# Retention and a bilinear feed-forward layer: seven short products instead of twelve long ones for three more pairs of output tiles

## The chip, the cores and the metric

One core of one Trainium2 chip runs the whole program. The metric is the device time of one execution in microseconds (us), as the median of several runs. The engines are TensorE (PE, matmuls; its weight loads are shown as PEld), VectorE (DVE), ScalarE (ACT), GpSimd (POOL) and SyncE (SP, which here only issues transfers).

## What is computed

A decaying recurrence over the sequence (a linear attention) for each batch and head, then a feed-forward layer that multiplies two projections with each other before the output projection:

```
state = gamma * state + k[t] (outer) v[t]           # 4 batches, 8 heads, 768 positions, 64 wide
y[t]  = (q[t] @ state) / sqrt(64)
x     = y, with the heads side by side              # (3072, 512)
out   = ((x @ w_a) * (x @ w_b)) @ w_out             # 512 -> 1536 -> 512, float32 out
```

## The kernel before

The 3072 rows are 24 tiles of 128 positions. They are gathered into eight groups, `TILES = [4, 2, 2, 2, 2, 4, 4, 4]`, called J = 0 to 7. For a group the kernel computes the hidden rows in twelve blocks `ft` of 128 of the 1536 hidden columns: `ffn_a` (four matmuls with w_a into a PSUM bank, which ACT casts to `asb`), `ffn_g` (four matmuls with w_b into another bank, which DVE multiplies with `asb` into `ht`). Then the output of the group is made, by tile (`ffn_out`) or by pair of tiles (`ffn_fast`).

`ffn_out(J, i)` (line 617) makes one tile: twelve matmuls with 512 columns of w_out each, a copy of the bank by ACT into `osb`; after the second tile of a pair `osb` is put on the list `held`, which the next `store()` sends out.

`ffn_fast(J, u)` (line 663) makes a pair of tiles u at once by Strassen's scheme in Winograd's form: with the rows of the pair and the two halves of w_out as a 2x2 matrix, seven products of half the width replace eight. A product is six matmuls of 256 columns (`product`, line 652). Its left side is either hidden rows as they are ("h") or one of four sums of hidden rows ("s", tiles `hsum`, made by `add` on DVE); its right side is either w_out (`wo_bf`) or one of four combinations of its quarters (`wt_bf`, made by `combine_o` on DVE). In the text the products are called by their left sides: h00, h10, h11 (no sum) and s1, s0, s2, s3. The before runs them in the order h00, h10, s1, s0, s2, s3, h11. Three banks are used: R1 takes h00, s1, s2, h11 one upon the other; R6 takes h10; R5 takes s0, s3. Between products that go into one bank ACT copies a state of it into `snap`. So s2 cannot begin before ACT has copied s1's result, nor s3 before s0's.

In the before `FAST = (2, 3, 5, 6, 7)`: groups 2, 3, 5, 6 and 7 run `ffn_fast`, groups 0, 1 and 4 run `ffn_out`. The sums of a fast group are made during its own blocks by the table `adds`.

The recurrence is laid between these. `turn(new, old)` (line 393) makes on PE the chunk states and scores of two new tiles and the results y of two older ones: some 130 small matmuls. Its chunk states go to one of the three banks of the pool `psff`, which the blocks and the output use too (lines 274 to 299); DVE adds them up (`sums`, four instructions, the first and third of which read that bank), and only then is the bank free. The casts of its results into `xt` (ACT, line 383) and of the states into `gst` (ACT, line 199) are put on a list `later`, from which `catch_up(n)` issues n at a time; the masking of scores (DVE, line 320) is on a list `unmasked`, issued by `mask_now(n)`. `casts(t)` scales keys and queries of a tile on POOL (line 236), then issues their transposing transfer on SP and the loads of the next two tiles. The table `ahead` says where each of these stands: at a block (J, ft) or at an output tile (J, "o", i); `visit` issues it.

The order of all instructions of an engine is fixed by the order in which the code is written (`seq`). A buffer of a pool is given to the next tile in the order in which the earlier ones are done in that order. SBUF tiles `wstage` (four of tag wa, four of tag wb) hold in turn the raw weights, then `osb`, `hsum` and `snap`.

Of the kernel before, what the change touches and what calls it, by code (L numbers as in the profile page):

```python
# [9 lines left out]
F32 = mybir.dt.float32  # L10
# [6 lines left out]
FAST = (2, 3, 5, 6, 7)  # L17
# [7 lines left out]
def kernel(  # L25
# [10 lines left out]
    nc = tc.nc  # L36
# [533 lines left out]
    def ffn_a(J, ft, c0=0, c1=None):  # L570
# [5 lines left out]
        for kt in range(KT):  # L576
            for b0, b1 in parts(J, ft, c0, c1, NFT):
# [6 lines left out]
    def ffn_g(J, ft, c0=0, c1=None):  # L584
# [3 lines left out]
        for kt in range(KT):  # L588
            for b0, b1 in parts(J, ft, c0, c1, NFT):
# [5 lines left out]
    def ffn_ab(J, ft):  # L595
        if ft > 1:
            store()
        ffn_a(J, ft)
        ffn_g(J, ft)
        catch_up(TILES[J] // 2)  # L600
        mask_now(1)
# [38 lines left out]
    def add(J, which, f0, f1):  # L640
        if J not in hsum:
            hsum[J] = [wstage.tile([P, NH, 2, P], BF16, tag="w" + "ab"[i % 2], name="hsum") for i in range(4)]
        s = [x[:, f0:f1, : TILES[J] // 2] for x in hsum[J]]
        x, y, op = {
            0: (lambda: rows(J, 0, 1, f0, f1), lambda: rows(J, 1, 1, f0, f1), ALU.add),
            1: (lambda: s[0], lambda: rows(J, 0, 0, f0, f1), ALU.subtract),
            2: (lambda: rows(J, 0, 0, f0, f1), lambda: rows(J, 0, 1, f0, f1), ALU.subtract),
            3: (lambda: rows(J, 1, 0, f0, f1), lambda: s[1], ALU.subtract),
# [14 lines left out]
    def ffn_fast(J, u):  # L663
        osb, dst = placed[J, u] = place(J, u)
        ends = J == len(TILES) - 1 and u == TILES[J] // 2 - 1
        snap = wstage.tile([P, 3, DH], F32, tag="w" + "ba"[u % 2], name="snap")
# [3 lines left out]

        R1 = bank()
        product(R1, J, u, ("h", 0, 0), (0, 0), True)
        seq(nc.scalar.copy(snap[:, 0], R1[:, :DH]))  # L673
        catch_up(2)
        R6 = bank()
        product(R6, J, u, ("h", 1, 0), (0, 2), True)
        seq(nc.vector.tensor_tensor(osb[:, 0, :DH], R6[:, :DH], snap[:, 0], op=ALU.add))
        mask_now(1)
        catch_up(1)
        store()  # L680
        product(R1, J, u, ("s", 1), (1, 1), False)
        seq(nc.scalar.copy(snap[:, 1], R1[:, :DH]))
# [8 lines left out]
        if ends:  # L691
            seq(nc.sync.dma_start(out=dst[:, 1, DH:], in_=osb[:, 1, DH:]))
        product(R5, J, u, ("s", 3), (0, 3), False)
        seq(nc.vector.tensor_tensor(osb[:, 0, DH:], R5[:, :DH], snap[:, 1], op=ALU.add))
        mask_now()
        if ends:
            seq(nc.sync.dma_start(out=dst[:, 0], in_=osb[:, 0]))
        catch_up(1)
        product(R1, J, u, ("h", 1, 1), (1, 3), False)
        seq(nc.scalar.copy(osb[:, 1, :DH], R1[:, :DH]))  # L700
        if J < len(TILES) - 2:
            held.append((dst, osb))
        elif ends:
# [126 lines left out]
    def visit(*at):  # L830
        for fn, *what in ahead.pop(at, []):
            fn(*what)
# [56 lines left out]
```

## Time and profile before

| what | us |
|---|---|
| median of 3 runs (222.60, 224.06, 227.06) | 224.06 |
| the profiled execution | 223.43 |
| its span, from the first to the last instruction | 221.5 |
| PE busy in it | 213.6 (96%) |
| DVE busy | 132.1 (60%) |
| ACT busy | 94.6 (43%) |
| POOL busy | 81.2 (37%) |
| mean granted TensorE clock | 0.997 |

The profiled execution took 1.93 us more than its span. A line of the timeline has the start in us from the span's start, the length in us, the engine, the line of the kernel, the operation, the tiles (written <- read), the shape and how many such instructions in a row are merged; in brackets stands the idle time of the engine before it and what ended it. Matmuls are pipelined, so the length of a merged row reaches over the start of the next; the time that a stretch takes on PE is read from start to start. The outputs stand at these places: groups 0 and 1 from 51.2 to 68.9 us, group 2 from 80.8, group 3 from 97.6, group 4 from 114.5, group 5 from 143.1, group 6 from 178.4, group 7 from 208.5.

### The profile page before, as it was taken

The numbers are of one execution on the slowest core, as the hardware profiler recorded it, in microseconds if no ns is written. First come the engines' busy times: TensorE is split into PE (matmuls) and PEld (weight loads), VectorE is DVE, ScalarE is ACT, GpSimd is POOL, SyncE is SP. The second block draws the span as 40 slices with busy tenths as digits, with TensorE's granted clock in tenths as the row PEclk, the third lists the DMA queues.
The fourth block names the chain that finished last, engine by engine and source line by source line (L and its number), as shares of the span: only waits on it lengthen the run. The fifth ranks groups of instructions, "written<-read, shape, count | busy, mean of one in ns | idle before, by whom it ended". The sixth has DMA issues, their size and how long they took to land.

```text
span 221.5 us, 6783 instructions
## 1 busy us (share of the span) xinstructions
PE 213.6 (96%) x2809; PEld 149.4 (67%) x2809; DVE 132.1 (60%) x299; ACT 94.6 (43%) x220; POOL 81.2 (37%) x107
## 2 busy tenths in 40 slices
PE   8799999999999999999999999998999999999993
PEld 7578888885456888888875445576445488444682
DVE  2783556648615885787574358875357882355731
ACT  3775244342527445445465333625332633333231
POOL 6557798682734535054351606345000000000000
PEclk9999999999999999999999999999999999999998
DMA  6999999998998999997998979599400002200022
GB/s 175 344 377 382 368 293 376 345 203 165 220 265 185 211 211 222 133 227 201 211 142 188 229 160 232 116 249 164 195 0 3 0 3 95 98 0 1 0 98 95
DMA packets 94830, 39.76 MB, mean 180 GB/s; under 512 B 76112, under 2 KB 91728, under 8 KB 94800
## 3 DMA queue, kind: packets, MB, share of 16 engines
q1 hardware_dynamic: 94656, 39.20, 71.0%
q8 instruction: 22, 0.36, 0.7%
q10 hardware_dynamic: 144, 0.13, 0.2%
q14 instruction: 8, 0.07, 0.1%
HBM read 28.31 MB, written 6.29 MB: 156 GB/s over the span
## 4 chain that ended last, share of the span: by engine, by line
PE 85%; DMA 5%; ACT 3%; DVE 3%; POOL 1%; issue 1%; SPq 0%; ACTq 0%; POOLq 0%; DVEq 0%
PE g L590 28%; PE a L578 28%; PE o L660 13%; PE o L627 9%; DMA kf<-in_k_dram 3%; DMA out_dram<-osb 2%; ACT xt L383 1%; POOL kqb L236 1%; PE y L356 1%; PE at L314 1%; PE y L368 1%; DVE ht L593 1%; PE st L284 1%; DVE hsum L650 1%; PE tp L436 1%
## 5 line engine op out<-in xcount | busy, mean ns | idle before, releaser
L593 DVE TENSOR_TENSOR ht<-g,asb 128x256 bf16<-128x256 f32 (+1 forms) x98 | 53.8, 549 | 55.2 <-PE g L590 46.6
L590 PE MATMUL g<-xt,wb_bf 128*128 128x256 bf16 (+1 forms) x432 | 77.9, 308 | 0.1
L578 PE MATMUL a<-xt,wa_bf 128*128 128x256 bf16 (+1 forms) x432 | 77.6, 308 | 0.1
L582 ACT CAST asb<-a 128x256 bf16<-128x256 f32 (+1 forms) x98 | 46.2, 473 | 66.5 <-PE a L578 65.4
L590 PEld LDWEIGHTS <-wb_bf 128*128 128x128 bf16 x432 | 42.1, 98 | 20.6 <-issue 0.3
L578 PEld LDWEIGHTS <-wa_bf 128*128 128x128 bf16 x432 | 41.7, 98 | 20.1
L236 POOL TENSOR_TENSOR kqb<-kf,ktab 128x512 bf16<-128x512 f32 x21 | 22.8, 1088 | 39.3 <-DMA kf<-in_k_dram 30.8
L236 POOL TENSOR_TENSOR kqb<-qf,qtab 128x512 bf16<-128x512 f32 x21 | 22.5, 1071 | 6.1 <-DMA qf<-in_q_dram 5.8
L660 PEld LDWEIGHTS <-hsum 128*128 128x128 bf16 x192 | 18.6, 98 | 4.7 <-issue 1.7
L627 PE MATMUL o<-wo_bf,ht 128*128 128x512 bf16 x96 | 21.6, 379 | 0.0
L201 POOL CAST vb<-vf 128x512 bf16<-128x512 f32 x24 | 14.7, 623 | 17.1 <-DMA vf<-in_v_dram 11.2
L660 PE MATMUL o<-wt_bf,hsum 128*128 128x256 bf16 x144 | 17.7, 272 | 1.5 <-ACT snap L673 0.8
L627 PEld LDWEIGHTS <-ht 128*128 128x128 bf16 x96 | 9.2, 98 | 10.3
L660 PEld LDWEIGHTS <-ht 128*128 128x128 bf16 x144 | 13.7, 97 | 3.0 <-issue 0.2
L298 DVE TENSOR_TENSOR sums<-st,sums 128x256 f32<-128x256 f32 x30 | 12.7, 424 | 1.6
L199 ACT CAST gst<-sums 128x256 bf16<-128x256 f32 x33 | 12.5, 419 | 0.5 <-DVE sums L296 0.3
L650 DVE TENSOR_TENSOR hsum<-ht 128x256 bf16<-128x256 bf16 (+1 forms) x36 | 12.0, 339 | 0.4
L320 DVE TENSOR_TENSOR aT<-at,mask 128x512 bf16<-128x512 f32 x18 | 12.0, 680 | 0.0
L660 PE MATMUL o<-wo_bf,ht 128*128 128x256 bf16 x96 | 11.8, 273 | 0.0
L630 ACT COPY osb<-o 128x512 f32<-128x512 f32 x8 | 4.7, 586 | 12.1 <-PE o L627 11.4
L383 ACT CAST xt<-y 128x512 bf16<-128x512 f32 x16 | 8.7, 594 | 1.4 <-PE y L368 1.4
L700 ACT COPY osb<-o 128x256 f32<-128x256 f32 x8 | 3.0, 372 | 12.2 <-PE o L660 12.2
(83 smaller groups left out, 178.5 us busy)
## 6 DMA issues: line engine op xcount, KB each, us to landing
out_dram<-osb SPq DMA_DIRECT2D x11, 512.0 KB, 3.7
kf<-in_k_dram SPq DMA_DIRECT2D x18, 256.0 KB, 4.1
qf<-in_q_dram SPq DMA_DIRECT2D x36, 128.0 KB, 3.7
vf<-in_v_dram SPq DMA_DIRECT2D x18, 256.0 KB, 4.2
wsta<-in_moe_w_a_dram SPq DMA_DIRECT2D x6, 512.0 KB, 7.6
wstb<-in_moe_w_b_dram SPq DMA_DIRECT2D x6, 512.0 KB, 7.7
wsto<-in_moe_w_out_dram SPq DMA_DIRECT2D x6, 512.0 KB, 9.3
kf<-in_k_dram SPq DMA_DIRECT2D x3, 512.0 KB, 6.0
```

Of the source, the lines that this page charges most:

```text
L199: seq(nc.scalar.copy(dst, src))
L201: seq(engine.tensor_copy(dst, src))
L236: seq(eng.tensor_tensor(dst, src, tab, op=ALU.mult))
L298: seq(nc.vector.tensor_tensor(new, u[c][:, s], old, op=ALU.add))
L320: unmasked.append(lambda r=r: seq(nc.vector.tensor_tensor(aT[n][:, r].rearrange("p s h d -> p (s h) d"), at[:, r].rearrange("p s h d -> p ...
L578: seq(nc.tensor.matmul(a[:, b0 - c0 : b1 - c0], wa_bf[:, kt, fs], xcols(J, kt, b0, b1), start=(kt == 0 and b0 == c0), stop=(kt == KT - 1 a ...
L582: seq(nc.scalar.copy(asb, a))
L590: seq(nc.tensor.matmul(g[:, b0 - c0 : b1 - c0], wb_bf[:, kt, fs], xcols(J, kt, b0, b1), start=(kt == 0 and b0 == c0), stop=(kt == KT - 1 a ...
L593: seq(nc.vector.tensor_tensor(ht[J][:, ft, c0:c1], g, asbs.pop((J, ft, c0)), op=ALU.mult))
L627: seq(nc.tensor.matmul(o, ht[J][:, ft, i * P : (i + 1) * P], wo_bf[:, f, 2 * r : 2 * r + 2, :].rearrange("p a d -> p (a d)"), start=(ft == ...
L650: seq(nc.vector.tensor_tensor(s[which], x(), y(), op=op))
L660: seq(nc.tensor.matmul(R[:, :DH], lhs, (wo_bf, wt_bf)[w][:, f, m, :], start=(first and f == 0), stop=(f == NH - 1), skip_group_check=True))
```

## The change

Five things, all in the order and kind of instructions; what is computed stays the same but for rounding.

1. `ffn_fast` also makes the second pair of group 0 (tiles 2, 3), the pair of group 1 and the pair of group 4. Only the first pair of group 0 keeps `ffn_out`.
2. In every fast pair but the last of all, h11 is made third, into a bank of its own (R4), before any product with a sum; ACT copies it into a fourth part of `snap`. The last DVE instruction on R1 then writes both halves of a row block at once (128x512, with the bank read twice). The ACT copy of the last product falls away.
3. The sums for groups 0 and 1: four `add` of 128x768 behind the first pair of group 0 (they share their tiles with group 1), and four more of 128x768 for group 1, two in front of and two behind the end of group 0's second pair. Group 4 makes its sums in its blocks as groups 2 and 3 do.
4. `visit(J, "o", 2u + 1)` is now called inside `ffn_fast`: behind h11, or for group 1 behind s0. With it the turns of groups 1, 4 and 5 stand inside a pair; that of group 5 moves from between its pairs into the first pair.
5. `store()` stands in `blocks`, ahead of `visit`, and group 5 calls it from its first block on. Blocks 8 to 11 of group 0 use matmuls of 512 columns instead of twice 256.

```diff
-FAST = (2, 3, 5, 6, 7)
...
-            for b0, b1 in parts(J, ft, c0, c1, NFT):
+            for b0, b1 in parts(J, ft, c0, c1, 8):
...
     def ffn_ab(J, ft):
-        if ft > 1:
-            store()
...
-    def add(J, which, f0, f1):
+    def add(J, which, f0, f1, u0=0):
...
-        snap = wstage.tile([P, 3, DH], F32, tag="w" + "ba"[u % 2], name="snap")
+        snap = wstage.tile([P, 4, DH], F32, tag="w" + "ba"[u % 2], name="snap")
...
+        def keep(i, R):
+            seq(nc.scalar.copy(snap[:, i], R[:, :DH]))
+        def plus(dst, R, x):
+            seq(nc.vector.tensor_tensor(dst, R[:, :DH], x, op=ALU.add))
         R1 = bank()
         product(R1, J, u, ("h", 0, 0), (0, 0), True)
-        seq(nc.scalar.copy(snap[:, 0], R1[:, :DH]))
+        keep(0, R1)
         catch_up(2)
-        R6 = bank()
+        R2 = bank()
...
+        plus(osb[:, 0, :DH], R2, snap[:, 0])
         mask_now(1)
         catch_up(1)
         store()
+        if not ends:
+            R4 = bank()
+            product(R4, J, u, ("h", 1, 1), (1, 3), True)
+            keep(2, R4)
+            if J != 1:
+                visit(J, "o", 2 * u + 1)
         product(R1, J, u, ("s", 1), (1, 1), False)
-        seq(nc.scalar.copy(snap[:, 1], R1[:, :DH]))
+        keep(1, R1)
         catch_up(1)
         R5 = bank()
         product(R5, J, u, ("s", 0), (1, 0), True)
-        seq(nc.scalar.copy(snap[:, 2], R5[:, :DH]))
+        keep(3, R5)
+        if J == 1:
+            visit(J, "o", 2 * u + 1)
         catch_up(1)
         product(R1, J, u, ("s", 2), (1, 2), False)
-        seq(nc.vector.tensor_tensor(osb[:, 1, DH:], R1[:, :DH], snap[:, 2], op=ALU.add))
+        if ends:
+            plus(osb[:, 1, DH:], R1, snap[:, 3])
+            seq(nc.sync.dma_start(out=dst[:, 1, DH:], in_=osb[:, 1, DH:]))
+        else:
+            seq(nc.vector.tensor_tensor(osb[:, 1].rearrange("p (c d) -> p c d", c=2),
+                                        R1[:, :DH].rearrange("p (c d) -> p c d", c=1).to_broadcast([P, 2, DH]),
+                                        snap[:, 2:], op=ALU.add))
         mask_now(1)
         product(R5, J, u, ("s", 3), (0, 3), False)
...
-        product(R1, J, u, ("h", 1, 1), (1, 3), False)
-        seq(nc.scalar.copy(osb[:, 1, :DH], R1[:, :DH]))
...
-        (0, "o", 3): [(casts, 9, "kq"), (casts, 8, "v"), (casts, 9, "v")],
+        (0, "o", 3): [(casts, 9, "kq"), (casts, 8, "v"), (casts, 9, "v"),
+                      (add, 1, 0, 0, NFT // 2), (add, 1, 1, 0, NFT // 2)],
...
-        (5, "o", 2): [(turn, 20, 18, D_), (casts, 23)],
+        (5, "o", 1): [(turn, 20, 18, D_), (casts, 23)],
...
     def blocks(J):
         for ft in range(NFT):
+            if ft > 1 or J == 5:
+                store()
             visit(J, ft)
...
-            if J not in FAST:
+            if J == 0 and i < 2:
                 ffn_out(J, i)
-                mask_now(2)
-                if (J, i) in combined:
-                    combine_o(*combined[J, i])
+                combine_o(3 * i, 3 * i + 3)
+                if i == 1:
+                    for which in range(4):
+                        add(0, which, 0, NH, 1)
+                    hsum[1] = hsum[0]
             elif i % 2 == 0:
...
                 ffn_fast(J, i // 2)
+                if J == 0:
+                    add(1, 2, 0, NH)
+                    add(1, 3, 0, NH)
```

The lines of the changed kernel are one lower than those of the before up to the blocks (L284 is L283). First place: DVE during the outputs of groups 0 and 1. `wt_bf` rows are the last two combinations of w_out, `sums` the state sums of a turn, `aT` the masked scores. Before:

```order
L217 TENSOR_TENSOR wt_bf<-wo_bf 128x3x256
L217 TENSOR_TENSOR wt_bf<-wo_bf,wt_bf 128x3x256
L296 COPY sums<-st 128x256
L298 TENSOR_TENSOR sums<-st,sums 128x256 x3
L320 TENSOR_TENSOR aT<-at,mask 128x512 x2
L333 COPY mark<-bq 128x1
```

Now:

```order
L216 TENSOR_TENSOR wt_bf<-wo_bf,wt_bf 128x3x256
L652 TENSOR_TENSOR hsum<-ht 128x6x128
L652 TENSOR_TENSOR hsum<-hsum,ht 128x6x128
L652 TENSOR_TENSOR hsum<-ht 128x6x128
L652 TENSOR_TENSOR hsum<-ht,hsum 128x6x128
L295 COPY sums<-st 128x256
L297 TENSOR_TENSOR sums<-st,sums 128x256 x3
L677 TENSOR_TENSOR osb<-o,snap 128x256
L319 TENSOR_TENSOR aT<-at,mask 128x512
L652 TENSOR_TENSOR hsum<-ht 128x6x128
L652 TENSOR_TENSOR hsum<-hsum,ht 128x6x128
L709 TENSOR_TENSOR osb<-o,snap 128x512
```

The four sums of hidden rows now stand in front of the state sums, whose third instruction frees the bank that h11 of the next pair is given.

Second place: ACT in the pair of group 3, from the copy of h00 on (`snap` rows are the copies between products, `xt` and `gst` come from the list `later`). Before:

```order
L383 CAST xt<-y 128x2x8x32 x2
L199 CAST gst_157<-sums 128x256
L682 COPY snap<-o 128x256
L199 CAST gst_158<-sums 128x256
L686 COPY snap<-o 128x256
```

Now:

```order
L382 CAST xt<-y 128x2x8x32 x2
L198 CAST gst_157<-sums 128x256
L674 COPY snap<-o 128x256 x2
L198 CAST gst_158<-sums 128x256
L674 COPY snap<-o 128x256
```

One copy more, that of h11, stands in front of the copies on which s2 and s3 wait; the copy at the pair's end is gone.

Third place: DVE in the first pair of group 5, whose turn has moved in (`mark` is the instruction by which the turn waits for its own first matmuls). Before:

```order
L677 TENSOR_TENSOR osb<-o,snap 128x256
L689 TENSOR_TENSOR osb<-o,snap 128x256
L694 TENSOR_TENSOR osb<-o,snap 128x256
L333 COPY mark<-bq 128x1
L298 TENSOR_TENSOR sums<-st,sums 128x256 x4
```

Now:

```order
L652 TENSOR_TENSOR hsum<-ht,hsum 128x256 x2
L677 TENSOR_TENSOR osb<-o,snap 128x256
L332 COPY mark<-bq 128x1
L297 TENSOR_TENSOR sums<-st,sums 128x256 x4
L709 TENSOR_TENSOR osb<-o,snap 128x512
```

The turn's mark stands behind the pair's last sums of hidden rows instead of behind the whole pair.

More of the change, by code (lines that the diff above doesn't have):

```diff
@@ L588, in ffn_g @@
         for kt in range(KT):
-            for b0, b1 in parts(J, ft, c0, c1, NFT):
+            for b0, b1 in parts(J, ft, c0, c1, 8):
                 seq(nc.tensor.matmul(g[:, b0 - c0 : b1 - c0], wb_bf[:, kt, fs], xcols(J, kt, b0, b1),
@@ L703, in ffn_fast @@
         elif ends:
+            seq(nc.sync.dma_start(out=dst[:, 0], in_=osb[:, 0]))
+            product(R1, J, u, ("h", 1, 1), (1, 3), False)
+            seq(nc.scalar.copy(osb[:, 1, :DH], R1[:, :DH]))
             seq(nc.scalar.dma_start(out=dst[:, 1, :DH], in_=osb[:, 1, :DH]))
@@ L830, in visit @@
     def visit(*at):
-        for fn, *what in ahead.pop(at, []):
+        for fn, *what in ahead.pop(at, ()):
             fn(*what)
```

30 lines of the change are left out of this document (14 added, 16 removed).

## The prediction

> **What bounds the kernel now.** I read the page first (busy shares and the clock row), then the timeline at every output stage, then who held DVE there. PE is busy throughout, at full clock; the other engines only count where PE stops for them.
>
> ```profile
> PE 213.6 (96%) x2809; PEld 149.4 (67%) x2809; DVE 132.1 (60%) x299; ACT 94.6 (43%) x220; POOL 81.2 (37%) x107
> PEclk9999999999999999999999999999999999999998
> ```
>
> So a gain must shorten PE's list or remove one of its few stops, and a new stop counts in full. Next, the outputs on PE. The starts of the rows matter; lengths overlap, and rows between those shown are left out here and below. First the long form, in the stage of groups 0 and 1: three tiles from 57.18, the turn from 65.05, a tile from 66.32, the first block of group 2 at 68.92.
>
> ```profile
> 57.18 7.94 PE L627 MATMUL o<-wo_bf,ht 128*128 128x512 bf16 x36
> 65.05 0.28 PE L356 MATMUL y<-kqT,gst 64*64 64x64 bf16 x10
> 66.32 2.76 PE L627 MATMUL o<-wo_bf,ht 128*128 128x512 bf16 x12
> 68.92 0.60 PE L578 MATMUL a<-xt,wa_bf 128*128 128x256 bf16 x4
> ```
>
> A tile costs 68.92 - 66.32 = 2.60 us, a pair 5.20; the turn between costs 66.32 - 65.05 = 1.27. Now the short form: the second pair of group 6, which nothing disturbs, then groups 2 and 3 and the two pairs of group 5.
>
> ```profile
> 183.07 1.47 PE L660 MATMUL o<-wo_bf,ht 128*128 128x256 bf16 x12
> 187.74 1.03 PE L578 MATMUL a<-xt,wa_bf 128*128 128x512 bf16 x4
> 80.82 1.48 PE L660 MATMUL o<-wo_bf,ht 128*128 128x256 bf16 x12
> 85.76 0.60 PE L578 MATMUL a<-xt,wa_bf 128*128 128x256 bf16 x4
> 97.61 1.48 PE L660 MATMUL o<-wo_bf,ht 128*128 128x256 bf16 x12
> 102.59 0.60 PE L578 MATMUL a<-xt,wa_bf 128*128 128x256 bf16 x4
> 143.11 1.47 PE L660 MATMUL o<-wo_bf,ht 128*128 128x256 bf16 x12
> 148.53 0.28 PE L356 MATMUL y<-kqT,gst 64*64 64x64 bf16 x10
> 149.74 1.48 PE L660 MATMUL o<-wo_bf,ht 128*128 128x256 bf16 x12
> 155.60 1.03 PE L578 MATMUL a<-xt,wa_bf 128*128 128x512 bf16 x4
> ```
>
> Undisturbed, 42 matmuls take 187.74 - 183.07 = 4.67 us, so a product is 0.66 (two thirds of a microsecond) and a pair in the short form saves 5.20 - 4.67 = 0.53. The others lose to stops: group 2 (4.94) 0.27, group 3 (4.98) 0.31, group 5 (5.42 and 5.86) 0.75 and 1.19. That is all there is to win: 3 x 0.53 + 2.52 = 4.1 us, under 2% of 223.43. What is in front of it is DVE's list.
>
> **Part 1: groups 0 and 1.** The new sums fall where DVE is full and POOL is active.
>
> ```profile
> 55.35 0.55 DVE L217 TENSOR_TENSOR wt_bf<-wo_bf,wt_bf 128x768 bf16<-128x768 bf16 x1
> 55.47 1.33 POOL L236 TENSOR_TENSOR kqb<-kf,ktab 128x512 bf16<-128x512 f32 x1 [3.94 <-DMA kf<-in_k_dram]
> 57.00 0.42 DVE L296 COPY sums<-st 128x256 f32<-128x256 f32 x1 [1.10 <-PE st L284]
> 57.53 1.34 DVE L298 TENSOR_TENSOR sums<-st,sums 128x256 f32<-128x256 f32 x3
> 57.79 1.04 POOL L236 TENSOR_TENSOR kqb<-qf,qtab 128x512 bf16<-128x512 f32 x1 [0.98 <-DMA qf<-in_q_dram]
> 58.79 1.28 DVE L320 TENSOR_TENSOR aT<-at,mask 128x512 bf16<-128x512 f32 x2
> ```
>
> In the before DVE runs its eighth combination to 55.90 and is free when the state sums come at 57.00. Now four sums of 128x768 stand between. Their price is that of the combination, the same shape and type: 0.55 each, 0.47 from start to start. If that were all, they would end at 55.82 + 0.47 x 3 + 0.55 = 57.8. But DVE instructions of this kind are held by POOL's:
>
> ```profile
> 132.25 0.42 DVE L650 TENSOR_TENSOR hsum<-ht 128x512 bf16<-128x512 bf16 x1
> 133.88 1.04 POOL L236 TENSOR_TENSOR kqb<-qf,qtab 128x512 bf16<-128x512 f32 x1
> 133.98 1.23 DVE L650 TENSOR_TENSOR hsum<-ht,hsum 128x512 bf16<-128x512 bf16 x1
> 80.22 1.10 POOL L236 TENSOR_TENSOR kqb<-kf,ktab 128x512 bf16<-128x512 f32 x1 [5.19 <-PE st L284]
> 80.46 1.02 DVE L650 TENSOR_TENSOR hsum<-hsum,ht 128x256 bf16<-128x256 bf16 x1
> ```
>
> Each was begun just after a POOL scaling and ended 0.29 and 0.16 us behind the end of that; undisturbed, the first would have taken the 0.42 of the row at 132.25. The state sums at 57.53, which read PSUM, were not held. The Trainium skill says the same (SBUF — State Buffer, "SBUF: two separate sides"): two-input VectorE work in SBUF and GpSimd work take a shared port pair in turn, the later fully blocked; the rows above agree. By that rule alone, with the rows' durations, the sum is the one that follows; without it, it would be the rival "sums not held".
>
> Step by step on this clock: the first sum is held until POOL ends at 56.80 and ends about 57.2; the second and third end at 57.7 and 58.2; POOL's scaling of 57.79 goes next, to 59.2; the fourth sum ends about 59.6. The third state sum, which frees the bank, ended in the before 57.53 + 2/3 x 1.34 - 57.00 = 1.43 us after their start: now 61.05. PE meanwhile begins h00 at 57.18 and is through h10 at 57.18 + 2 x 0.66 = 58.5. h11, third, is given just this bank, so PE stands until 61.05: 2.55 us. Bounds: 59.2 - 58.5 = 0.7 (sums not held) and 3.6 (POOL also goes ahead of the third sum, one more scaling of 1.04). I take the middle, since the scaling at 57.79 is ready then in the trace.
>
> Behind h11 the rest follows without a long stop. The prices on DVE and ACT there, a 128x512 instruction with PSUM as its source among them:
>
> ```profile
> L593 DVE TENSOR_TENSOR ht<-g,asb 128x512 bf16<-128x512 f32 x46 | 31.8, 691 | 36.6 <-PE g L590 34.4 <-PE st L477 0.9 <-ACT asb L582 0.9
> L677 DVE TENSOR_TENSOR osb<-o,snap 128x256 f32<-128x256 f32 x8 | 3.3, 418 | 4.3 <-PE o L660 3.4 <-ACT snap L673 0.9
> 81.73 0.37 ACT L673 COPY snap<-o 128x256 f32<-128x256 f32 x1 [1.67 <-PE o L660]
> 82.00 1.08 ACT L383 CAST xt<-y 128x512 bf16<-128x512 f32 x2
> ```
>
> DVE then has the state sums (0.42 + 1.34), the addition on h10 (0.42), a mask (0.64), two sums of group 1 (1.0, one perhaps held), the double-width last addition (0.69), mask and addition (1.1): done at about 65.6, and h11 of group 1 needs the last bank at 57.18 + 2.55 + 9 x 0.66 = 65.7. I add 0.75 for the small ones: ACT's copies in front of s2 and s3, and the casts of `xt` from the turn of group 1, which now has only two products, 1.3 us, behind it to cover two casts of 0.54 and their wait, with the first block's second bank behind the double-width addition. The next block begins at 57.18 + 14 x 0.66 + 1.27 + 2.55 + 0.75 = 71.0 instead of 68.92: **+2.1** (0 to +4: 1.05 more by the upper bound, and up to 1 if group 1's own sums are each held).
>
> **Part 2: groups 2 and 3.** h11 third gives the sums 0.66 us more, but its bank is the turn's, and its copy stands in front of the two copies that bound these pairs.
>
> ```profile
> 81.40 1.32 DVE L298 TENSOR_TENSOR sums<-st,sums 128x256 f32<-128x256 f32 x3
> 83.26 0.40 ACT L682 COPY snap<-o 128x256 f32<-128x256 f32 x1
> 97.30 0.29 DVE L650 TENSOR_TENSOR hsum<-hsum,ht 128x256 bf16<-128x256 bf16 x1
> 99.29 1.19 POOL L236 TENSOR_TENSOR kqb<-kf,ktab 128x512 bf16<-128x512 f32 x1
> ```
>
> In the before s1's copy ends at 83.66, which holds s2 for the 0.27. Five products now end at 80.82 + 5 x 0.66 = 84.1, so that wait goes; but the bank comes free at 82.72 where h11 could begin at 82.14. The hidden sum held at 80.46 makes it so late. With such a hold the stop moves: 0.58 and about 0.1 for s0's copy, against 0.27: +0.4; without it, -0.27. POOL is paced by its loads and PE will be 2 us later, so whether they meet is a draw: group 2 **0** (-0.3 to +0.4), group 3 **+0.3** (-0.3 to +0.7; its second hidden sum, at 97.30, moves 2 us later onto the POOL scaling at 99.29).
>
> **Part 3: group 4.** The pair saves 0.53; of it ACT's copy for s3, behind a cast of `xt` of 0.54 that now comes inside the pair, takes some 0.2: **-0.3** (-0.5 to 0). Its sums ride in DVE's gaps, as those of groups 2 and 3 do.
>
> **Part 4: group 5.** Two stops of the before:
>
> ```profile
> 134.95 5.91 SPq L249 DMA_TRANSPOSE kqT<-kqb  x2
> 144.51 1.03 DVE L650 TENSOR_TENSOR hsum<-hsum,ht 128x256 bf16<-128x256 bf16 x1
> 146.78 0.91 SPq L607 DMA_DIRECT2D out_dram<-osb  x1
> 151.57 0.37 ACT L673 COPY snap<-o 128x256 f32<-128x256 f32 x1 [2.57 <-DMA out_dram<-osb]
> 152.00 2.37 PE L660 MATMUL o<-wt_bf,hsum 128*128 128x256 bf16 x18 [0.77 <-ACT snap L673]
> ```
>
> The first copy of the second pair waits for the store of group 4, issued on SP only at 146.78, behind eight loads; its buffer is the store's. Now that store stands in front of the transposes of tiles 20 and 21 (134.95) and goes out some 12 us earlier: 0.77, the wait shown, to 1.19, all that this pair loses, are won. In the first pair s1 no longer waits for the held sum (0.75), but the turn's mark now stands behind these sums and their addition on DVE, and PE cannot pass the mark: about 0.75 to 1.0 is lost again there. Net **-0.9** (-1.9 to -0.3). On SP the store passes two transposes and eight loads, each 0.9 us later; the turn needs them some 3 us sooner than before, which POOL's pace still allows.
>
> Part 5: in blocks 8 to 11 of group 0, 64 matmuls of 256 columns become 32 of 512; by the rows above a 512 takes 2.60 / 12 = 0.217 and two of 256 2 x 4.67 / 42 = 0.222: -0.1. Groups 6 and 7 run at 4.7 a pair already: 0, and the tail stays as it was.
>
> **The sum.** +2.1 + 0 + 0.3 - 0.3 - 0.9 - 0.1 = +1.1 on 223.43, the profiled execution: **224.5 us**. The median of the runs, 224.06, is 0.6 above that execution, so I call this no change that a measurement tells: about 2%, 4.5 us, is what it can tell here.
>
> **Rivals.**
> (a) The sums are not held, since POOL's loads land otherwise: groups 0 and 1 end even (+0.1), groups 2 and 3 win 0.3 each, group 4 0.3, group 5 1.4: 223.43 - 2.2 = 221.2, faster than before. It decides if the first state sum begins before 58.0. For it: the gaps of POOL are long (3.94 before 55.47). Against: its instruction at 55.47 lies right over the first sum. Chance 0.27.
> (b) One scaling more and group 1's sums held too: +4.1 in groups 0 and 1, +0.7 in group 3, the rest as forecast: 223.43 + 3.5 = 227.0. Chance 0.17.
> (c) The clock. A stop of up to 3.6 us, where the longest single one quoted above is 0.77, could lower PE's clock; if it fell to half for the five products behind the stop, they would take 6.6 instead of 3.3 us: 224.5 + 3.3 = 227.8, with (b) 230. The clock row shows full speed through all the stops of this trace, which says nothing of one this long. Chance 0.06. The Trainium skill (TensorE: Matmul & The Clock Gate, "HAM oscillation") has such a rule, for idle gaps over about 3.4 us; no run here shows one.
> (d) The short form wins nothing because ACT's copies bound every new pair as they bound groups 2 and 3, and the early store wins nothing: 223.4. Chance 0.10, inside the forecast's range.
> The forecast itself: 0.40, from 223.4 to 225.8.
>
> Range: from (a) to a little above (b), leaving 0.2 out: 221.2 to 227.4. Faster by over 2% (under 219.0) needs more than every gain above: 0.03. Slower by over 2% (over 227.9) is (b) at its bound or (c): 0.09. Within: 0.88.
>
> **What would show it.** In the changed profile: the first `sums` of the turn behind group 0's first pair beginning at about 59.6 instead of 57.00, and PE idle before the third product there, 2 to 3 us, put down to DVE; a sum of 128x768 with a length over 1 us beside a POOL scaling; the first block of group 2 at 71; pairs of groups 2 and 3 near 5.0; no wait of ACT for a store in group 5, and a wait of PE on `mark` in its turn. If PE does not stop behind h10 of group 0, the main term is wrong and (a) holds; if the clock row dips near 61 us, (c).

## The result, and the profile after

The changed kernel takes 231.05 us, the median of four runs (230.71 to 231.64), against 225.56 for the kernel before beside it (222.60 to 227.80, four runs): 1.035 times as long, 95% interval 1.028 to 1.042. The forecast was 224.5 and the range ended at 227.4. Ratios here and below leave out runs that stood over 1.5% above the fastest of their kernel; medians take all of them.

The profiled execution took 230.98 us, its span 229.3. The page's busy shares and clock row:

```profile
PE 214.3 (93%) x2831; PEld 151.9 (66%) x2831; DVE 149.8 (65%) x328; ACT 95.6 (42%) x226; POOL 82.4 (36%) x107
PEclk9999999999889999999999999999999999999999
```

PE's busy time grew by 0.7 us and the span by 7.8, so most of the loss is stops. The clock row, full in the before but for its last slice, in which PE ends, has two slices of 8, from 57 to 69 us. The starts of rows on PE give the stages. The columns before and after are one execution each; the last column has the least and the most that the stage takes in the profiles of the before and of those experiments below that leave it, and for blocks the output of the group ahead of them, as in the before:

| stage, from start to start | before | after | forecast | came | unchanged, over the profiles |
|---|---|---|---|---|---|
| outputs of groups 0 and 1, to the first block of group 2 | 17.71 | 22.95 | +2.1 | +5.24 | 17.71 to 19.18 |
| blocks of group 2 | 11.90 | 12.68 | none named | +0.78 | 11.77 to 12.46 |
| pair of group 2 | 4.94 | 5.75 | 0 | +0.81 | 4.89 to 5.44 |
| blocks of group 3 | 11.85 | 13.14 | none named | +1.29 | 11.85 to 12.42 |
| pair of group 3 | 4.98 | 4.64 | +0.3 | -0.34 | 4.90 to 5.62 |
| blocks of group 4 | 11.92 | 13.50 | none named | +1.58 | 11.85 to 11.94 |
| output of group 4 with its turn | 6.50 | 6.27 | -0.3 | -0.23 | 6.50 to 6.60 |
| blocks of group 5 | 22.10 | 22.21 | none named | +0.11 | 22.10 to 22.64 |
| pairs of group 5 with the turn | 12.49 | 11.98 | -0.9 | -0.51 | 10.94 to 12.49 |

The sum under "came" is +8.73; the first stage begins 0.62 sooner and groups 6 and 7 take 0.31 less, which leaves the 7.8 of the spans. The first stage and the blocks of groups 3 and 4 stand clear of the spread between executions; the -0.51 of group 5 does not.

The timeline of the first stage (columns as before), DVE against POOL, then PE:

```profile
55.01 1.17 POOL L235 TENSOR_TENSOR kqb<-kf,ktab 128x512 bf16<-128x512 f32 x1 [4.09 <-DMA kf<-in_k_dram]
55.20 1.40 DVE L652 TENSOR_TENSOR hsum<-ht 128x768 bf16<-128x768 bf16 x1
56.55 1.04 POOL L235 TENSOR_TENSOR kqb<-qf,qtab 128x512 bf16<-128x512 f32 x1 [0.37 <-DMA qf<-in_q_dram]
56.63 1.38 DVE L652 TENSOR_TENSOR hsum<-hsum,ht 128x768 bf16<-128x768 bf16 x1
57.55 1.35 POOL L235 TENSOR_TENSOR kqb<-kf,ktab 128x512 bf16<-128x512 f32 x1
57.93 1.39 DVE L652 TENSOR_TENSOR hsum<-ht 128x768 bf16<-128x768 bf16 x1
58.87 1.35 POOL L235 TENSOR_TENSOR kqb<-qf,qtab 128x512 bf16<-128x512 f32 x1
59.25 1.39 DVE L652 TENSOR_TENSOR hsum<-ht,hsum 128x768 bf16<-128x768 bf16 x1
60.56 0.41 DVE L295 COPY sums<-st 128x256 f32<-128x256 f32 x1
61.08 1.34 DVE L297 TENSOR_TENSOR sums<-st,sums 128x256 f32<-128x256 f32 x3
...
62.02 1.46 PE L662 MATMUL o<-wt_bf,ht 128*128 128x256 bf16 x6 [3.98 <-DVE sums L297]
63.28 2.95 PE L662 MATMUL o<-wt_bf,hsum 128*128 128x256 bf16 x18
...
66.72 1.47 PE L662 MATMUL o<-wo_bf,ht 128*128 128x256 bf16 x12
...
73.54 0.60 PE L577 MATMUL a<-xt,wa_bf 128*128 128x256 bf16 x4
```

All four hidden sums are held, one for one with POOL's four scalings, which now come nearly back to back (0.37 of idle time between the first two). The state sums begin 4.00 us after PE's start on the pair (56.56) instead of 0.18 ahead of it, and h11 waits 3.98 us for the bank. Then h11 itself takes 63.28 - 62.02 = 1.26 us instead of 0.66. The windows view by microseconds has the reason (PE busy, PEld, DVE, ACT, POOL, and then the granted clock):

```profile
61.00:62.00 1.00, 0.00 (x0) 0.00 (x0) 0.85 (x3) 0.81 (x3) 0.52 (x1) 0.76 1.00 264
62.00:63.00 1.00, 0.98 (x5) 0.73 (x6) 1.00 (x3) 0.40 (x1) 1.00 (x3) 0.50 1.09 389
...
64.00:65.00 1.00, 1.00 (x7) 0.70 (x6) 0.41 (x1) 0.20 (x1) 0.00 (x0) 0.53 0.58 131
65.00:66.00 1.00, 1.00 (x11) 0.90 (x10) 0.00 (x0) 0.85 (x3) 0.00 (x0) 1.00 1.21 273
```

The clock is halved from 61.52 (0.76 is half speed for 0.48 of that microsecond) to 64.94: 3.42 us. Five products of 0.66 take 66.72 - 62.02 = 4.70 us instead of 3.3, which is 1.4 lost.

In the blocks two patterns recur. At the start of group 4's blocks (the end of the pair of group 3):

```profile
109.36 0.69 DVE L709 TENSOR_TENSOR osb<-o,snap 128x512 f32<-128x512 f32 x1 [1.03 <-ACT gst L198]
109.97 0.68 DVE L319 TENSOR_TENSOR aT<-at,mask 128x512 bf16<-128x512 f32 x1
110.57 0.41 DVE L677 TENSOR_TENSOR osb<-o,snap 128x256 f32<-128x256 f32 x1
110.86 0.60 PE L577 MATMUL a<-xt,wa_bf 128*128 128x256 bf16 x4
110.90 0.42 DVE L592 TENSOR_TENSOR ht<-g,asb 128x256 bf16<-128x256 f32 x1
```

Four matmuls of a block take 0.44 from start to start; those ahead of 110.86 began at 110.19, so PE stood 0.24. With h11 no longer at the pair's end, the double-width addition, a mask and the last addition, 1.78 us, stand on DVE in front of the next block's multiplication. And near the end of group 4's blocks:

```profile
120.61 1.04 POOL L235 TENSOR_TENSOR kqb<-qf,qtab 128x512 bf16<-128x512 f32 x1
120.70 1.10 DVE L652 TENSOR_TENSOR hsum<-hsum,ht 128x256 bf16<-128x256 bf16 x1
120.78 0.60 PE L589 MATMUL g<-xt,wb_bf 128*128 128x256 bf16 x4
121.73 0.41 DVE L592 TENSOR_TENSOR ht<-g,asb 128x256 bf16<-128x256 f32 x1
122.19 0.60 PE L577 MATMUL a<-xt,wa_bf 128*128 128x256 bf16 x4 [0.81 <-DVE ht L592]
```

Again a held sum, here of 128x256 (0.28 when free), in front of the `ht` that empties PE's bank: from start to start 122.19 - 120.78 = 1.41 us instead of 0.44, so 0.97 is lost.

### The profile page after: what moved, and what is told of

Read it like the earlier page. It is cut to its first block, busy times and chain, and to the rows that moved or that the text cites. A ratio compares the mean times of both kernels' runs of the same rounds, so it can differ in the third digit from the quotient of the medians.

```text
span 229.3 us, 6861 instructions
## 1 busy us (share of the span) xinstructions
PE 214.3 (93%) x2831; PEld 151.9 (66%) x2831; DVE 149.8 (65%) x328; ACT 95.6 (42%) x226; POOL 82.4 (36%) x107
## 4 chain that ended last, share of the span: by engine, by line
PE 80%; DVE 9%; DMA 4%; issue 3%; ACT 2%; POOL 1%; SPq 0%; DVEq 0%; ACTq 0%; POOLq 0%
PE a L577 27%; PE g L589 25%; PE o L662 21%; DVE hsum L652 5%; DMA kf<-in_k_dram 4%; DVE ht L592 2%; POOL kqb L235 1%; PE at L313 1%; PE y L355 1%; PE y L367 1%; PE st L283 1%; DVE sums L297 1%; PE tp L435 1%; PE st L476 1%; ACT asb L581 1%
## 5 line engine op out<-in xcount | busy, mean ns | idle before, releaser
L674 ACT COPY snap<-o 128x256 f32<-128x256 f32 x43 | 16.1, 374 | 31.5 <-PE o L662 28.7
L662 PEld LDWEIGHTS <-hsum 128*128 128x128 bf16 x264 | 26.0, 100 | 4.5 <-issue 0.8
L662 PEld LDWEIGHTS <-ht 128*128 128x128 bf16 x198 | 19.0, 99 | 9.7 <-DVE sums L297 5.5
L662 PE MATMUL o<-wt_bf,hsum 128*128 128x256 bf16 x198 | 24.6, 278 | 0.6 <-DVE osb L677 0.6
L652 DVE TENSOR_TENSOR hsum<-ht 128x256 bf16<-128x256 bf16 (+2 forms) x46 | 20.5, 452 | 0.5
L662 PE MATMUL o<-wo_bf,ht 128*128 128x256 bf16 x132 | 16.4, 273 | 0.8 <-DVE ht L592 0.8
L709 DVE TENSOR_TENSOR osb<-o,snap 128x512 f32<-128x512 f32 x10 | 6.9, 691 | 13.1 <-PE o L662 10.6
L662 PE MATMUL o<-wt_bf,ht 128*128 128x256 bf16 x66 | 9.7, 286 | 5.0 <-DVE sums L297 5.0
L677 DVE TENSOR_TENSOR osb<-o,snap 128x256 f32<-128x256 f32 x23 | 9.6, 416 | 3.6 <-ACT snap L674 1.9
L652 DVE TENSOR_TENSOR hsum<-ht,hsum 128x256 bf16<-128x256 bf16 (+2 forms) x23 | 11.4, 507 | 0.0
```

Source lines behind the costliest of these rows:

```text
L652: seq(nc.vector.tensor_tensor(s[which], x(), y(), op=op))
L662: seq(nc.tensor.matmul(R[:, :DH], lhs, (wo_bf, wt_bf)[w][:, f, m, :], start=(first and f == 0), stop=(f == NH - 1), skip_group_check=True))
L674: seq(nc.scalar.copy(snap[:, i], R[:, :DH]))
```

## The experiments

The theory after this reading: the loss in groups 0 and 1 is the stop behind sums that POOL's scalings hold, and the halved clock behind the stop; what is lost in groups 2 to 4 comes from h11 third (bank, and no cover at a pair's end) and from new sums in group 4's blocks. The rivals are that DVE's list is too long whether held or not, that the slow products have another cause, and that groups 2 to 4 only suffer from the shift.

### Groups 0 and 1 as before

```diff
-            if J == 0 and i < 2:
+            if J < 2:
                 ffn_out(J, i)
-                combine_o(3 * i, 3 * i + 3)
-                if i == 1:
-                    for which in range(4):
-                        add(0, which, 0, NH, 1)
-                    hsum[1] = hsum[0]
+                mask_now(2)
+                if J == 0 and i < 2:
+                    combine_o(3 * i, 3 * i + 3)
```

> The changed kernel, but groups 0 and 1 make all their tiles in the long form again, as before the change (no sums for them); groups 2 to 7 stay as changed. Theory (most of the loss is the stop behind the held sums and the low clock behind it): the stage of groups 0 and 1 takes 17.7 us again instead of 22.95, and the time is 231.05 - 5.2 = 225.8 us, 225 to 227 with what the moved transfers do to groups 2 to 4. Rival (the short form with h11 third costs as much in groups 2, 3 and 4 whatever went before): the stage loses only its own 5.2 and groups 2 to 4 keep their +3.4 on their spans, so 226 or more with pairs of 5.75 in group 2 and blocks of 13.1 and 13.5 in groups 3 and 4. Rival (groups 0 and 1 are not the cause): 229 or more.

Median 225.84 us (ten runs; the before beside it 223.49, nineteen runs), ratio 1.006 (1.002 to 1.010). The stage takes 68.67 - 50.96 = 17.71 again. So the short form in groups 0 and 1 is 5.2 us of the loss by the medians, 5.7 without the runs that the ratios leave out, and 5.24 in the stage table. The rest of the change alone still loses: in this profile group 2's pair takes 6.12, behind two held sums, and group 4's blocks 13.53. The pairs of groups 2 and 3 and the blocks behind them together take 3.70 us more than in the before here, 3.34 in the changed kernel, so this loss does not come from what groups 0 and 1 shift.

### POOL's scalings kept off the four sums

```diff
+        if (t, i) == (8, 0):
+            tc.add_manual_dep(bi.ins, last_add[0].name, after, reason="scaling behind the sums")
```

> The changed kernel, but POOL's first scaling of tile 8 waits for the fourth hidden sum of group 0, so that no scaling lies beside the four sums. Theory (the sums of 128x768 are slow only because POOL's scalings hold them): each takes 0.55 us instead of 1.39, the first state sum begins at about 57.2 instead of 60.56, PE stops about 0.9 us instead of 3.98 behind h10, the clock stays up, and the time is 231.05 - 3.1 - 1.4 = 226.5 us, less if POOL being later spares group 1, more if its scalings now meet the sums of group 1. Rival (the sums of hidden rows are slow by their own layout, or DVE's list is too long anyway): sums of 1.3 us or a stop of over 2.5 us remain and the time is 230 us or more.

Median 226.27 us (ten runs), ratio 1.008 (1.005 to 1.013). The timeline:

```profile
55.22 0.55 DVE L656 TENSOR_TENSOR hsum<-ht 128x768 bf16<-128x768 bf16 x1
...
56.75 0.55 DVE L656 TENSOR_TENSOR hsum<-ht,hsum 128x768 bf16<-128x768 bf16 x1
57.22 0.42 DVE L299 COPY sums<-st 128x256 f32<-128x256 f32 x1
57.43 1.04 POOL L235 TENSOR_TENSOR kqb<-kf,ktab 128x512 bf16<-128x512 f32 x1 [6.50 <-PE o L666]
...
58.67 0.83 PE L666 MATMUL o<-wt_bf,ht 128*128 128x256 bf16 x6 [0.61 <-DVE sums L301]
```

The four sums take 0.55 or 0.56 each, the stop is 0.61 us, the clock stays full, and the stage is 68.53 - 50.61 = 17.92. (POOL's wait is put down to PE in the view; the edit makes POOL wait for the fourth sum, which ends at 57.30.) That settles the first rival: the shape, the layout and the length of DVE's list were not the matter, POOL was. But with hardly any stop the short form still does not beat the long one there (17.71).

### The stop filled with matmuls

```diff
+        if J == 0:
+            warm(18, psat, "y1", 4 * P, wo_bf[:, 0].rearrange("p a d -> p (a d)"))
```

> The changed kernel, with 18 more matmuls of 512 columns whose result nobody uses on PE between h10 and h11 of group 0's second pair, some 3.9 us of work laid into the stop. Theory (the products behind the stop are slow, 1.26 instead of 0.66 us, since the clock was lowered because PE stood still): the clock row stays at 9 through the place, the products behind it take 0.66 each, and the time is 231.05 - 1.4 = 229.6 us. Rival (they are slow for another reason, waits for weights or for the sums): the clock makes no difference, 231 us.

Median 229.16 us (four runs, 226.78 to 231.71), ratio 1.015 (1.009 to 1.021). DVE is as late as in the changed kernel. PE in the profiled execution:

```profile
62.33 0.83 PE L662 MATMUL o<-wt_bf,ht 128*128 128x256 bf16 x6
...
65.62 1.47 PE L662 MATMUL o<-wo_bf,ht 128*128 128x256 bf16 x12
```

The clock row of its page has no dip:

```profile
PEclk9999999999999999999999999999999999999999
```

The five products take 65.62 - 62.33 = 3.29 us, as at full clock. So the 1.4 us belong to the clock and not to the sums or the weights. The times alone would not decide it: two of the four runs lie above the theory's 229.6, at 230.37 and 231.71. The profiled run is 4.2 us under that of the changed kernel, its first stage (71.55 - 51.00 = 20.55) only 2.40, so other stages differ too; these were not followed.

### Two sums ahead of the state sums, two behind

```diff
-                    for which in range(4):
+                    for which in range(2):
                         add(0, which, 0, NH, 1)
...
+                elif J == 0:
+                    add(0, 2, 0, NH, 1)
+                    add(0, 3, 0, NH, 1)
```

> The changed kernel, but only the sums for s1 and s0 stand in front of the state sums, the other two behind them. Theory (the stop is the time by which DVE comes late to the state sums that free the bank): two held sums of 1.4 us fewer stand in front, the first state sum begins at about 58.0 instead of 60.56, the stop is about 1.5 us instead of 3.98, the clock falls less or not at all, and the time is 231.05 - 2.4 - 0.7 to 1.4, so 227.2 to 228; a new wait of up to 1 us before s2 if the two sums behind are held too. Rival (the stop is not the bank but the sums that s1 needs): no change, 230 us or more.

Median 228.13 us; the four runs are 225.55 and 226.41 with a mean clock of 1.0, 229.85 and 229.90 with 0.993. In the profiled one (226.41) the stop is a third of what it was:

```profile
59.53 0.83 PE L662 MATMUL o<-wt_bf,ht 128*128 128x256 bf16 x6 [1.39 <-DVE sums L297]
```

So the stop is the time by which the sums delay the state sums, and the bank is what h11 waits for. The runs with the lower clock were not looked into.

### Group 5 alone, and its store alone

Both start from the kernel before. In the first, `ffn_seven` is `ffn_fast` of the changed kernel; the second has only the last of these edits.

```diff
     def ffn_fast(J, u):
+        if J in (5,):
+            return ffn_seven(J, u)
...
-        (5, "o", 2): [(turn, 20, 18, D_), (casts, 23)],
+        (5, "o", 1): [(turn, 20, 18, D_), (casts, 23)],
...
         for ft in range(NFT):
+            if J == 5:
+                store()
             visit(J, ft)
```

> The kernel before, with the change for group 5 alone: its store from the first block on, h11 third in its two pairs, the turn inside the first pair. The pairs of group 5 took 12.49 us before (143.11 to 155.60) and 11.13 to 12.13 in the changed kernel and four versions of it. Theory (the wait for the store goes, part of it is lost again at the turn's mark): those 12.49 us become 11.1 to 12.1 and the time is 0.4 to 1.4 us under that of the kernel before. Rival (the store and its wait only moved): the stretch stays at 12.5 and the time at that of the kernel before.

> The kernel before, with nothing changed but that group 5 sends the store of group 4 from its first block on instead of its third; the turn stays between the two pairs. Theory (the second pair of group 5 loses 1.19 us only because the first copy waits for that store): that pair takes 4.7 us instead of 5.86 and the time is 0.8 to 1.2 us under that of the kernel before. Rival (the store set the wait, but ACT's or DVE's other work ends just as late): no change, and the same wait of PE put down to another engine.

The kernel before stood at 223.27 beside these two and the next two. Group 5 alone: 223.57 us, ratio 1.002 (0.999 to 1.005), the pairs 155.22 - 143.33 = 11.89 instead of 12.49 in the profile of the before. The store alone: 223.05, ratio 0.999 (0.997 to 1.002). With the store alone the second pair takes 156.69 - 151.80 = 4.89 us instead of 5.86, without a wait for the store. But that does not show the early store at work. The version with the masks moved (below) leaves group 5 as in the before, and there:

```profile
151.35 1.48 PE L660 MATMUL o<-wo_bf,ht 128*128 128x256 bf16 x12
156.25 1.03 PE L578 MATMUL a<-xt,wa_bf 128*128 128x512 bf16 x4
```

The store is issued on SP at 146.74, as late as in the before (146.78), and the pair takes 4.90 us without a wait for it; PE comes to the pair 1.61 us later than in the profile of the before (149.74). All five versions with group 5 as it was (groups 2 and 3 alone, group 4 alone, the masks, the two with a stop) have 4.89 or 4.90. So the wait on which the prediction counts stands in one of the six profiles with this code, and what the early store is worth when PE comes early was not measured. By the intervals group 5 alone wins 0.2 us at most, the store alone 0.6, both less than the 0.9 of the prediction. The first pair of the version with the store alone still loses 0.78 to a held sum, and its first stage, which the edit does not touch, takes 19.18 us:

```profile
66.61 0.32 PE L314 MATMUL at<-kqT 64*64 64x64 bf16 x16 [0.81 <-DMA kqT<-kqb]
```

The turn of tiles 8 and 9 waits for its transposed tiles there, although the output is in the long form; in the profile of group 4 alone it waits 0.89.

### Group 4 alone, groups 2 and 3 alone

The kernel before with that `ffn_seven` for group 4 (with its sums), and for groups 2 and 3.

```diff
-FAST = (2, 3, 5, 6, 7)
+FAST = (2, 3, 4, 5, 6, 7)
...
     def ffn_fast(J, u):
+        if J in (4,):
+            return ffn_seven(J, u)
```

> The kernel before, with the change for group 4 alone: its pair in the short form with h11 third and the turn inside it, its sums made in its blocks. Theory (DVE's new sums in the blocks of group 4 make PE wait there, above all when POOL's scalings hold them): the blocks from the end of group 3's pair take 12.6 to 13.5 us instead of 11.92, the output with its turn about 6.0 to 6.5 instead of 6.50, and the time is 0.4 to 1.4 us over that of the kernel before. Rival (the prediction on record: the sums ride in gaps of DVE): blocks of 11.9 and 0.3 us under the kernel before.

> The kernel before, with h11 third in its own bank in the pairs of groups 2 and 3 alone. Theory (h11 third now waits for the bank that the state sums free, and without h11 at the end the last additions of a pair stand in front of the next block's on DVE): group 2's pair 5.3 to 6.1 us instead of 4.94, group 3's 4.6 to 5.3 instead of 4.98, the blocks behind each 0.3 to 0.6 longer, and the time is 0.8 to 2.3 us over that of the kernel before. Rival (the prediction on record): +0.3, between -0.6 and +1.1. Rival (the low order of the losses in groups 2 and 3 comes only from what groups 0 and 1 shift): no change.

Group 4 alone: 223.59 us, ratio 1.001 (0.998 to 1.004). Its blocks take 12.39 (116.75 - 104.36) instead of 11.92, its output 6.06 instead of 6.50: the two cancel. Neither the gain of the prediction nor the loss of the theory shows in the time. Groups 2 and 3 alone: 224.32, ratio 1.005 (1.003 to 1.008), some 1.2 us where the prediction had +0.3. PE waits 0.19 and 0.59 for the bank of h11, and loses 0.24 behind each pair, 0.60 more in group 3's blocks behind a sum held for 1.11.

### The masks behind the next block's multiplication

The version for groups 2 and 3, without the pair's own second mask (the blocks issue it):

```diff
                                         snap[:, 2:], op=ALU.add))
-        mask_now(1)
         product(R5, J, u, ("s", 3), (0, 3), False)
         plus(osb[:, 0, DH:], R5, snap[:, 1])
-        mask_now()
```

> The kernel before with h11 third in groups 2 and 3 (+0.53%, 0.27 to 0.79, when measured alone), but with the second mask of each of these two turns issued behind the next block's first multiplication instead of in front of it. Theory (without h11 at its end the pair's last additions and the mask stand on DVE in front of the next block's multiplication, and PE waits 0.25 us for a bank in the second block): that gap goes behind both pairs, and the time is about 0.5 us under that run, +0.3% over the kernel before; the waits for the bank of h11 stay. Rival (the gap is only moved one block on): +0.5% again.

Median 223.40 us, ratio 1.000 (0.997 to 1.003). After the pair of group 2:

```profile
85.74 0.69 DVE L707 TENSOR_TENSOR osb<-o,snap 128x512 f32<-128x512 f32 x1 [1.62 <-ACT gst L199]
86.13 0.60 PE L578 MATMUL a<-xt,wa_bf 128*128 128x256 bf16 x4
...
86.56 0.60 PE L590 MATMUL g<-xt,wb_bf 128*128 128x256 bf16 x4
87.00 0.60 PE L578 MATMUL a<-xt,wa_bf 128*128 128x256 bf16 x4
```

The next `a` begins 0.44 behind `g`: the gap is gone, and no block of groups 3 and 4 has one. So the lost cover was a part of the loss, as the trace shows; in the time the two intervals just touch (up to 1.003 here, from 1.003 with the mask in front). The pairs still have their waits (group 3's s0 1.16 here).

### The best of the parts

The kernel before with the early store, and groups 0 and 1 in the short form with POOL's scalings kept off the four sums of group 0 and the first two of group 1:

```diff
+        if (t, i) in ((8, 0), (9, 0)):
+            tc.add_manual_dep(bi.ins, last_add[0].name, after, reason="scaling behind the sums")
```

> What the experiments so far leave as the best of the parts: the kernel before, with the early store of group 5, and with groups 0 and 1 in the short form as changed, but with POOL's scalings kept off all their hidden sums (tile 8 behind the fourth sum of group 0, tile 9 behind the second sum of group 1); groups 2 to 7 otherwise as before. Theory (what POOL holds is the whole loss of groups 0 and 1): their stage took 17.92 us with the first four sums free and loses another 0.5 where the sums of group 1 were held, so about 17.4 instead of 17.71, and the time is 0.3 to 1.2 us under that of the kernel before. Rival (the turn of tiles 8 and 9 is bound by their loads, scalings and transposes, so a shorter output only waits there): a wait on the transposed tiles in that turn, a stage of 18 us or more, and 0 to 1.5 us over the kernel before.

Median 225.46 us (twelve runs; before 223.20, 23 runs), ratio 1.009 (1.006 to 1.013): slower, and not as expected. The stage takes 68.68 - 50.62 = 18.06, and the blocks of group 2 13.32 instead of 11.90:

```profile
67.52 1.07 ACT L387 CAST xt<-y 128x512 bf16<-128x512 f32 x2 [1.07 <-PE y L372]
68.68 0.27 PE L582 MATMUL a<-xt,wa_bf 128*128 128x256 bf16 x1
69.79 0.50 PE L582 MATMUL a<-xt,wa_bf 128*128 128x256 bf16 x3 [0.84 <-issue]
```

PE stops 1.00 us inside the first block, and 0.24 twice behind it. Three of group 1's four sums still take 0.85, 0.83 and 0.96 instead of 0.55, beside POOL's casts of values and its last scaling, and s0 of group 1 waits 0.47 for the addition behind them, so holds still cost something in the stage. No wait on a transposed tile is shown in this profile, so the rival did not come in it (in the long form it did in two, see above). What holds PE at 69.79 the profile does not say ("issue"). So the holds of sums are not the whole loss of groups 0 and 1; what else costs 1.4 us behind the turn of group 1 stays open (only two products now stand between it and the blocks, but that this is the cause was not tried). None of the versions beats the kernel before by more than its interval.

### A stop and nothing else

The kernel before; PE's third tile of group 0 waits for the state casts on ACT and one, or four, copies more.

```diff
+        if (J, i) == (0, 2):
+            for _ in range(1):
+                seq(nc.scalar.copy(idle_to, wo_bf[:, 0, :2].rearrange("p a d -> p (a d)")))
...
+            if (J, i, ft) == (0, 2, 0):
+                tc.add_manual_dep(bi.ins, last[mybir.EngineType.Activation].name, after, reason="stop")
```

> The kernel before, with one stop of PE added and nothing else: its third tile of group 0 waits for the casts of the states and one more copy on ACT, about 2.8 us. Theory (the clock falls only behind a stop longer than some length between 2.8 and 4 us): the clock row stays at 9, tiles behind the stop take 2.60 us, and the time is 2.8 us over that of the kernel before, less what the turn of tiles 8 and 9 had waited for its transfers anyway (up to 1). Rival (the clock goes down with any stop of some microseconds): a dip in the row and 4 to 4.5 us.

> The same with four such copies on ACT, a stop of about 4.5 us. Theory (a stop of this length lowers the clock for some microseconds behind it, as in the changed kernel, where 3.98 us of stop were followed by products of 1.26 instead of 0.66 us): the clock row dips behind the stop, the tile behind it takes over 3.5 us instead of 2.60, and the time is 4.5 + 1.5 to 2 = 6 to 6.5 us over that of the kernel before, less up to 1 in the turn. Rival (the low clock of the changed kernel had another cause, the work of the other engines for one): no dip, tiles of 2.60 us, 4.5 us.

The short one: 227.64 us, ratio 1.017 (1.011 to 1.024). The long one: 230.09, ratio 1.029 (1.023 to 1.034). The windows of the short one, with the clock as the third number from the end:

```profile
56.00:57.00 1.00, 1.00 (x60) 0.58 (x61) 0.00 (x0) 0.38 (x1) 0.83 (x1) 1.00 1.13 259
57.00:58.00 1.00, 0.27 (x28) 0.16 (x16) 0.85 (x2) 0.61 (x2) 0.00 (x0) 1.00 1.02 223
...
59.00:60.00 1.00, 0.09 (x1) 0.09 (x2) 1.00 (x2) 0.86 (x2) 1.00 (x2) 0.70 0.90 206
...
62.00:63.00 1.00, 1.00 (x4) 0.39 (x3) 0.00 (x0) 0.00 (x0) 0.87 (x2) 0.59 1.25 397
```

And of the long one, the first microsecond at half clock and the one in which it ends:

```profile
60.00:61.00 1.00, 0.00 (x0) 0.00 (x0) 0.00 (x0) 0.97 (x2) 0.55 (x1) 0.50 1.39 255
...
66.00:67.00 1.00, 1.00 (x4) 0.39 (x3) 0.00 (x0) 0.35 (x1) 0.71 (x1) 0.58 0.82 186
```

The stop of 2.64 us was enough: half clock from 59.40 to 62.82, and the three tiles behind it take 9.29 us (59.91 to 69.20) instead of 7.87, 1.42 more. So the expected length between 2.8 and 4 us was wrong. The stop of 4.59 us is followed by half clock from 60.00 to 66.84, and by tiles that take 2.71 more. The rival (another cause of the low clock in the changed kernel) falls: nothing was added here but a stop and the copies on ACT that make it.

## Why the prediction was wrong, point by point

**Groups 0 and 1 (+2.1, came +5.24).** The mechanism stood in the prediction: hidden sums in front of the state sums, held by POOL, and PE standing for the bank behind h10. Two terms were mis-sized. First, "the second and third end at 57.7 and 58.2": only the first and the fourth were taken as held, since POOL's scalings were laid where they stood in the before, the second 0.61 us behind PE's start on the pair (57.79 and 57.18). In the changed kernel its load came sooner: it began with the pair (56.55 and 56.56) and met the second sum, the third scaling followed at once and met the third, and each sum waited for one. Counted as the prediction counts, from 56.56 + 2 x 0.66 = 57.88, h11 began 4.14 us late (62.02) instead of 2.55: 1.59 more. Second, the clock was left out of the sum, as rival (c) with 0.06; measured, it is 1.4. The remaining 0.15 is in the small waits (0.75 forecast, about 0.9 came). Rival (c) joined with (b) has the right events but for group 1's sums, of which only one was held. That its 230 us is near the time is luck: it puts 4.1 + 3.3 = 7.4 into the first stage, where 5.24 came, and nothing into the blocks of groups 2 to 4, where 3.65 came.

**Groups 2 and 3 (0 and +0.3).** The pairs came at +0.81 and -0.34, each outside its bounds by under half a microsecond: which of them meets a held sum is indeed a draw (in the changed kernel and the four versions made from it these pairs take 4.85 to 6.12 and 4.60 to 6.07). The step that failed is one that was not there: nothing was said of the blocks behind a pair, whose cover h11 had been (0.24 each, and 1.2 us of time with the waits for the bank when done alone). The prediction named that cover for group 1 only.

**Group 4 (-0.3).** The pair is right (-0.23). "Its sums ride in DVE's gaps" is wrong: the blocks lost 1.58 in the changed kernel, 0.97 of it behind the held sum shown above, and 0.47 when done alone.

**Group 5 (-0.9).** The -0.51 lies inside its bounds, but that is no success of the steps. The term took the stops of one profiled execution, 1.19 us with the wait for the store among them, for stops of the kernel. The 12.49 of that execution is the longest of the six profiles with group 5 as in the before (10.94 to 12.49); in the six with the change the pairs take 11.13 to 12.13. The one step that is borne out is what is lost in the first pair: the turn waits 0.31 there, and the last matmul of h10 0.77 for an `ht` behind two held sums.

**The wide matmuls (-0.1) and groups 6, 7 (0).** The first stage began 0.62 sooner; versions without the wide matmuls began at 50.62 to 51.26, so that is spread between executions and was not put down to the change. The 0.31 less in the last two groups is the change: the pairs of group 6 take 9.18 us in all five profiles with h11 third there and 9.38 to 9.40 in the nine without, and group 7's output is some 0.1 shorter in the same way. The prediction had put this gain at nothing.

The Trainium skill's rule on the shared port (SBUF — State Buffer, "SBUF: two separate sides") is that the one which starts first has the ports for its whole length and the other is blocked; the sums of 1.38 to 1.40 us instead of 0.55 agree. It was weighed correctly and then applied to a time table of the kernel before. That sums and scalings take turns one for one is what these rows show.

## What to carry to other kernels

Where two engines exclude each other, don't price a new row by where the other engine's rows stood: take as the upper bound that each new row meets one, and give the load-paced engine's jitter the chance it has. A stop of PE near 3 us can cost itself and some 1.4 us more at half clock, so it belongs in the sum. A step taken from the end of a stage has a cover to be paid for in the next one. And a stop that stands in one profiled execution is a gain to be had only if a second execution shows it too.

## What the runs showed of the hardware that was not expected

In these three traces the clock falls and rises in steps of one length: half clock for 3.42 us behind stops of 2.64 and 3.98 us, for 6.84, twice as long, behind 4.59 (of the other runs with this stop two have much the same mean clock as its 0.984, and one 0.992, as behind a single step). It fell 2.1 us after PE had stopped in the first (59.40), 3.5 in the changed kernel, 3.3 in the last. In the 3.42 us ahead of the fall at 59.40 PE had still been busy for 1.29. The Trainium skill (TensorE: Matmul & The Clock Gate, "HAM oscillation") sets its rule at idle gaps over about 3.4 us. The Trainium skill (the same page, "What's actually happening") has a free-running window of that length, and the steps agree with it. But 2.64 us of standing were enough here, in three of four runs by their mean clocks (0.992, 0.991 and 0.989). The fourth run has 1.0 and yet takes 227.31 us, no less than the others; what else it lost is not known.
